# A fused attention and snake-MLP kernel whose whole order is exchanged, with its column sums taken from GpSimd back to TensorE

## The chip, the cores and the metric

The kernel runs on one core of a Trainium2 chip. The metric is the device time of one execution in microseconds (us), lower is better. Times are the median of three runs of the kernel before, 223.31 us (223.25 to 224.26).

## The reference

Eight batches of eight heads, 512 positions of 64 numbers, and 32 state rows for each head. Two attentions share their scores, and an MLP with a snake activation follows on all 4352 rows.

```python
def _attn_ref(x, state):                       # x 8x8x512x64, state 8x8x32x64
    scores = scale * np.matmul(x, state.transpose(0, 1, 3, 2))
    a = softmax(scores, -1);  xread = np.matmul(a, state)
    scores2 = scale * np.matmul(state, x.transpose(0, 1, 3, 2))
    a2 = softmax(scores2, -1);  sread = np.matmul(a2, x)
    return np.concatenate([xread, sread], axis=2)
def _moe_ref(x, w_in, w_out, alpha):           # x 4352x512, w_in 512x2048, w_out 2048x512
    h = x @ w_in
    s = np.sin(alpha * h)
    g = h + s * s / (alpha + 1e-09)
    return g @ w_out
```

## The kernel before

The core has five engines that run beside each other, each through its own list of instructions in order: TensorE (PE in the profile; its weight loads are PEld), VectorE (DVE), ScalarE (ACT), GpSimd (POOL), and SyncE (SP), which only issues DMAs here. An instruction that waits holds up everything behind it on its own engine. PE writes into PSUM, which has eight banks; a bank can be written anew once its last reader is done.

The kernel is a list of some 1,580 small steps, the text `ORDER`, written out by a search program. Each step is a method of the class `Steps`. There is no scheduler behind it: the steps are issued as they stand, so each engine gets its own steps in the order of the list. Steps of different engines that stand side by side in the list need not run at the same time.

A step is written as name, numbers, engine. `sq.3.8.A` is the step `sq` for batch 3 and column tile 8 on ScalarE (A; V is VectorE, G is GpSimd). Batches are numbered 0 to 7; the number 8 stands for the 256 state rows of all batches, which go through the MLP last. The 2048 hidden columns are 16 tiles f of 128. The steps that matter here, with their lines in the profile:

- `li`, `lo` (L287, L299): the four quarters of `w_in` and of `w_out` are loaded and made bf16, by DMAs that GpSimd issues. `lx.b` (L280): batch b of `x`, 512 KB in bf16, the same way. `pk.b` (L353): two copies that reorder it; both need the whole of `lx.b`. `td.b` (L394): a DMA on SP that transposes it.
- `sc` (L404): scores, two halves g of a batch. `ex` (L411): their exponential E on ScalarE. `rs`, `rr` (L415, L421): row sums and reciprocals on VectorE. `nm` (L205): the normalised scores A on GpSimd. `ad.b` (L445): a DMA on SP that transposes A of batch b into AT.
- `m.b.s` and `me` (L507, L515): M, the state of batch b times a quarter s of `w_in`, in two PSUM banks, and their two copies into SBUF. So the first matrix product of the MLP is AT times M, without xread ever being formed.
- `h.t.f.bank` (L556, two matmuls; `hg`, L574, is one of them; L562 for batch 8, four matmuls of half the width): hidden tile f of batch t. `si` (L582): its sine on ScalarE. `sq` (L205, or L591 on ScalarE): the square. `gt` (L598): the gate gT on VectorE, which reads the PSUM bank of h for the last time.
- `oo.t.st.bank` takes a bank, and `o.t.st.f` (L611) is one of the 16 matmuls that add up an output tile in it; `oc` (L619) copies it out and `os` (L626, L629) stores it by a DMA on SP. The last output tile, `oh.7.3`, is made in two pieces of 384 and 128 columns.
- `w.b` (L472, L480), `rc`, `xs` (L487, L490): the other attention. E is used unnormalised; its column sums over the 512 positions of a batch are needed beside it, spread over two halves of the partitions (r is 0 or 1).

The column sums are where the code differs. Before, GpSimd first adds the four token blocks of E: `ca` adds two pairs in float32 (L453), `cb` adds the results (L457), `ch` and `cl` split the sum in a high and a low bf16 part (L461, L465). Then four matmuls in `w` (L480) with a 128-column weight of zeros and ones, `sel`, add over the partitions.

```python
        for r in range(2):
            for p in range(2):
                Ev = k.t["hilo", b][:, p].rearrange("p g (h r j) -> p g h r j", h=2, r=2)
                k.nc.tensor.matmul(
                    wc[:, :, 2 * k.Ns:], k.sel[:, (1 - r) * k.D:(3 - r) * k.D], Ev[:, :, :, r],
                    start=(r == 0 and p == 0), stop=(r == 1 and p == 1),
                )
```

Of the kernel before, what the change touches and what calls it, by code (L numbers as in the profile page):

```python
# [10 lines left out]
ALU = mybir.AluOpType  # L11
AX = mybir.AxisListType
BF16 = mybir.dt.bfloat16
FP32 = mybir.dt.float32
U32 = mybir.dt.uint32
# [7 lines left out]
zero.1 identf.V lq.3.S s01_c.G s01_t.0 s01_k.1.A s01_k.0.V xq.0.V xq.1.A warm_up.4.512.7 xtq.1.0  # L23
l_st xtq.0.1 xq.2.V xq.3.V li.0 li.1 xc.0.0.0.V li.2 xtq.2.2 xc.0.1.0.V lo.0 xtq.3.3 lo.1 xc.0.0.1.A
sc.0.0.1 lx.1.0.1 xc.0.1.1.A li.3 ex.0.0 warm_up.1.512.7 sc.0.1.3 lo.2 ex.0.1 warm_up.1.512.7
st_t.1.1 rs.0.0 rr.0.0 nm.0.0.0.4.G ho.0.1.3 rs.0.1 rr.0.1 st_c.1.1.A st_c.1.0.V al_t.2 st_t.0.0
st_c.0.0.A warm_up.3.512.7 at.0.0.4 st_c.0.1.V m.0.0.1.5 sin_table ac.0.0.V me.0.0.0.V me.0.0.1.A
m.1.0.0.6 me.1.0.0.A nm.0.1.0.4.G at.0.1.4 ac.0.1.V lo.3 ho.0.3.7 hg.0.3.0 al_c inva hg.0.3.1 si.0.3
me.1.0.1.V lx.2.0.1 sq.0.3.V hg.0.1.0 hg.0.1.1 ho.0.2.0 hg.0.2.1 m.0.1.2.4 me.0.1.1.V si.0.1
sq.0.1.V me.0.1.0.A hg.0.2.0 si.0.2 sq.0.2.G ho.0.0.6 m.1.1.5.1 me.1.1.0.A hg.0.0.0 hg.0.0.1  # L30
ho.0.6.4 hg.0.6.1 gt.0.3 si.0.0 sq.0.0.G hg.0.6.0 me.1.1.1.A ho.0.5.2 hg.0.5.0 gt.0.1 hg.0.5.1
m.0.2.7.5 me.0.2.1.A gt.0.2 ho.0.7.3 hg.0.7.1 me.0.2.0.V ho.0.4.1 hg.0.4.1 hg.0.7.0 m.1.2.0.5 si.0.6
sq.0.6.G gt.0.0 me.1.2.1.A me.1.2.0.V hg.0.4.0 si.0.4 gt.0.6 sq.0.4.V gt.0.4 ho.0.10.7 hg.0.10.0
si.0.5 sq.0.5.G si.0.7 sq.0.7.G hg.0.10.1 ho.0.9.5 hg.0.9.1 hg.0.9.0 gt.0.5 ho.0.11.6 hg.0.11.0
oo.0.0.0 o.0.0.2 o.0.0.3 o.0.0.0 ca.0 cb.0 ch.0 hg.0.11.1 si.0.11 sq.0.11.V oo.0.3.4 o.0.3.1 o.0.3.3
si.0.9 sq.0.9.A o.0.3.2 o.0.3.0 o.0.0.1 oo.0.2.1 o.0.2.0 o.0.2.1 o.0.0.4 o.0.3.4 oo.0.1.2 o.0.1.2
o.0.1.6 o.0.0.6 o.0.1.4 o.0.1.1 o.0.3.6 o.0.2.3 gt.0.7 o.0.3.7 ho.0.8.3 hg.0.8.1 hg.0.8.0 o.0.3.5
gt.0.11 gt.0.9 si.0.10 sq.0.10.A gt.0.10 xt.1.1.5 xc.1.1.0.V xt.1.0.7 cl.0 si.0.8 pk.1.0.V
xc.1.0.1.V xc.1.0.0.V o.0.1.5 o.0.2.4 o.0.1.7 o.0.2.7 sq.0.8.A gt.0.8 xc.1.1.1.A sc.1.1.5 ex.1.1
o.0.2.5 m.0.3.7.6 me.0.3.0.V o.0.0.5 o.0.2.2 o.0.1.3 sc.1.0.3 ex.1.0 ho.0.15.7 o.0.2.6 me.0.3.1.V  # L40
hg.0.15.0 pk.1.1.V o.0.0.7 m.1.3.5.6 me.1.3.1.A rs.1.1 rr.1.1 nm.1.1.0.4.G hg.0.15.1 rs.1.0 rr.1.0
ho.0.13.3 hg.0.13.1 si.0.15 o.0.3.8 o.0.2.11 me.1.3.0.V o.0.3.11 o.0.0.10 hg.0.13.0 o.0.3.9
nm.1.0.0.4.G ad.1 o.0.1.10 sq.0.15.V o.0.2.8 o.0.0.8 gt.0.15 ho.0.14.5 o.0.1.8 hg.0.14.0 hg.0.14.1
ho.0.12.6 hg.0.12.1 hg.0.12.0 o.0.3.10 o.0.1.11 o.0.2.10 o.0.1.15 o.0.1.9 si.0.13 sq.0.13.G o.0.2.15
gt.0.13 lx.3.0.1 o.0.3.15 o.0.0.15 o.0.0.13 o.0.3.13 o.0.2.9 o.0.1.13 si.0.14 sq.0.14.A gt.0.14
o.0.0.14 o.0.0.11 si.0.12 sq.0.12.A o.0.2.14 o.0.1.14 o.0.0.9 gt.0.12 o.0.0.12 h.1.1.6 oc.0.0.A
h.1.15.5 pk.2.1.V pk.2.0.V td.2 si.1.1 si.1.15 h.1.14.0 si.1.14 sq.1.14.G h.1.12.3 sq.1.1.V o.0.3.12
sq.1.15.V h.1.6.7 o.0.1.0 si.1.12 gt.1.1 o.0.1.12 oc.0.1.A o.0.2.12 gt.1.15 si.1.6 o.0.3.14
sq.1.12.V oc.0.3.A h.1.13.6 sq.1.6.G si.1.13 h.1.2.2 o.0.2.13 oc.0.2.A h.1.4.5 si.1.4 si.1.2
pk.3.0.V oo.1.1.4 o.1.1.15 gt.1.14 gt.1.12 gt.1.6 o.1.1.1 sq.1.13.G sq.1.4.V lx.4.0.1 oo.1.2.0  # L50
o.1.2.14 o.1.2.1 o.1.2.15 o.1.1.12 h.1.7.3 si.1.7 sq.1.2.G sq.1.7.A h.1.11.7 h.1.9.1 o.1.1.14
gt.1.13 o.1.1.13 si.1.11 sq.1.11.G h.1.8.6 gt.1.4 o.1.1.4 oo.1.3.5 o.1.3.6 o.1.3.4 o.1.3.13 o.1.3.15
gt.1.7 o.1.3.7 si.1.9 gt.1.2 si.1.8 sq.1.8.G sq.1.9.A h.1.5.3 si.1.5 gt.1.11 o.1.3.1 h.1.10.2
si.1.10 gt.1.9 o.1.2.6 gt.1.8 sq.1.5.G os.0.2 o.1.2.13 os.0.1 h.1.3.7 o.1.1.9 si.1.3 h.1.0.1 si.1.0
sc.2.0.6 o.1.1.2 sq.1.10.G o.1.2.2 o.1.2.8 sq.1.3.G o.1.3.2 gt.1.5 o.1.2.9 o.1.2.7 ex.2.0 pk.3.1.V
o.1.3.8 o.1.1.7 gt.1.10 o.1.3.5 sc.2.1.2 ex.2.1 o.1.1.5 gt.1.3 o.1.2.12 rs.2.0 ca.1 o.1.2.4 rr.2.0
m.2.3.7.6 me.2.3.1.A me.2.3.0.A nm.2.0.0.4.G rs.2.1 rr.2.1 nm.2.1.0.4.G os.0.0 m.2.2.2.3 td.3
sq.1.0.A me.2.2.1.V o.1.2.10 cb.1 ch.1 o.1.2.3 me.2.2.0.A gt.1.0 o.1.1.3 oo.1.0.6 o.1.0.6 o.1.0.10
o.1.3.9 o.1.0.11 w.0.7 ad.2 o.1.0.5 o.1.2.11 rc.0 xs.0.0 o.1.0.3 xs.0.1 o.1.0.14 o.1.0.12 o.1.2.0
o.1.1.8 o.1.2.5 oc.1.2.V m.2.0.1.2 me.2.0.0.A m.2.1.7.3 me.2.0.1.V o.1.1.10 o.1.3.0 o.1.0.13  # L60
pk.4.1.V o.1.0.7 cl.1 pk.4.0.V me.2.1.0.A me.2.1.1.A sc.3.1.1 o.1.3.12 sc.3.0.7 ex.3.1 rs.3.1
o.1.3.11 rr.3.1 nm.3.1.0.4.G ex.3.0 rs.3.0 o.1.0.2 o.1.3.10 h.2.14.1 si.2.14 o.1.1.11 rr.3.0 td.4
nm.3.0.0.4.G o.1.1.6 o.1.3.3 o.1.3.14 h.2.6.7 oc.1.3.V o.1.1.0 h.2.15.3 oc.1.1.V si.2.6 h.2.11.5
o.1.0.8 sq.2.6.G si.2.11 si.2.15 h.2.3.4 si.2.3 sq.2.14.V gt.2.14 h.2.1.2 si.2.1 o.1.0.1 sq.2.11.V
sq.2.15.G gt.2.6 gt.2.11 sq.2.1.G h.2.4.1 si.2.4 sq.2.4.G h.2.7.0 gt.2.15 sq.2.3.V si.2.7 o.1.0.9
gt.2.1 gt.2.3 o.1.0.4 o.1.0.0 os.1.3 o.1.0.15 oc.1.0.A h.2.13.7 si.2.13 oo.2.3.5 o.2.3.11 os.0.3
gt.2.4 o.2.3.6 sq.2.13.G gt.2.13 o.2.3.14 h.2.5.3 h.2.10.6 si.2.5 o.2.3.15 oo.2.1.2 o.2.1.6 o.2.1.15
sq.2.7.A si.2.10 o.2.1.1 sq.2.5.A h.2.9.4 si.2.9 ad.3 h.2.2.1 si.2.2 sq.2.2.A o.2.3.3 gt.2.7 gt.2.5
o.2.1.14 sq.2.10.G gt.2.10 h.2.12.7 sq.2.9.G gt.2.9 gt.2.2 w.1.0 h.2.8.3 o.2.3.5 o.2.3.13 o.2.1.4
o.2.1.13 o.2.1.5 sc.4.1.4 si.2.8 h.2.0.6 sq.2.8.A rc.1 si.2.12 si.2.0 oo.2.0.1 o.2.1.11 o.2.0.2  # L70
sq.2.12.V o.2.0.3 o.2.3.7 o.2.0.10 o.2.0.4 o.2.0.13 gt.2.12 o.2.0.9 o.2.3.1 gt.2.8 ex.4.1 xs.1.0
o.2.3.12 o.2.0.14 sq.2.0.G o.2.0.12 xs.1.1 o.2.3.9 m.3.0.4.3 m.3.1.0.7 o.2.1.2 ca.2 me.3.0.1.A cb.2
ch.2 gt.2.0 me.3.0.0.V o.2.3.4 o.2.3.8 me.3.1.1.A o.2.0.0 sc.4.0.4 o.2.3.10 ex.4.0 o.2.1.8
me.3.1.0.V m.3.3.0.7 m.3.2.3.6 rs.4.1 rr.4.1 h.3.0.4 o.2.3.0 o.2.0.5 me.3.3.0.V me.3.3.1.A o.2.0.1
nm.4.1.0.4.G o.2.0.6 me.3.2.1.A cl.2 o.2.1.0 me.3.2.0.V oo.2.2.3 o.2.2.14 o.2.2.3 rs.4.0 rr.4.0
si.3.0 h.3.12.6 si.3.12 nm.4.0.0.4.G o.2.3.2 h.3.8.0 o.2.0.7 h.3.9.7 oc.2.3.V sq.3.12.V gt.3.12
os.2.3 lx.5.0.1 si.3.8 sq.3.8.V si.3.9 gt.3.8 sq.3.0.V gt.3.0 h.3.4.5 sq.3.9.G gt.3.9 o.2.2.1 si.3.4
o.2.1.12 o.2.0.8 h.3.13.6 si.3.13 sq.3.13.A gt.3.13 o.2.1.9 o.2.2.7 sq.3.4.G o.2.2.6 os.1.2 gt.3.4
ad.4 o.2.2.0 h.3.3.0 si.3.3 o.2.0.11 o.2.0.15 o.2.1.10 oc.2.0.A sq.3.3.G gt.3.3 h.3.11.4 o.2.1.7
si.3.11 sq.3.11.G os.1.0 gt.3.11 o.2.1.3 o.2.2.5 oc.2.1.A os.2.1 h.3.7.1 si.3.7 sq.3.7.G o.2.2.8  # L80
m.4.3.6.7 me.4.3.1.V m.4.2.2.5 me.4.2.0.A pk.5.0.V gt.3.7 o.2.2.11 me.4.2.1.A h.3.15.0 si.3.15
o.2.2.15 me.4.3.0.A o.2.2.2 h.3.14.4 h.4.9.5 si.3.14 oo.3.3.7 sq.3.15.V gt.3.15 h.3.5.2 si.3.5
# [607 lines left out]
```

## Time and profile before

| what | before |
| --- | --- |
| median of 3 runs | 223.31 us (223.25 to 224.26) |
| the profiled execution, own time | 224.26 us |
| its span in the profile | 222.2 us |
| TensorE busy | 210.7 us, 95% of the span |
| VectorE busy | 179.3 us, 81% |
| ScalarE busy | 167.8 us, 76% |
| GpSimd busy | 109.9 us, 49% |
| granted TensorE clock, mean | 0.998 |
| DMA, mean | 106 GB/s |
| last matmul starts | 218.62 us after the start of the span |

The span is the time from the first to the last instruction of the program in one profiled execution; the device time has some 2 us around it. The profile names, for an engine's idle time, what ended it ("<-"). A mean over the whole span hides that this kernel has stages: up to 18 us it waits for weights, then it runs through the batches, and the end is a chain of output tiles.

### The profile page before, as it was taken

Reading aid. Unit: us, or ns where it says so; the run is one execution under the profiler, and the core shown is the slowest. Engines: PE = TensorE matmul, PEld = TensorE weight load, DVE = VectorE, ACT = ScalarE, POOL = GpSimd, SP = SyncE. Lnnn points to the kernel's source line nnn. Section 1 sums busy time; section 2 is a strip of 40 time slices with the busy share of each in tenths; the row PEclk is TensorE's granted clock in tenths of the full one; section 3 lists DMA queues with packets and bytes.
Section 4 is the critical chain, followed back from the end, with each engine's and each line's share of the span. In section 5 each row is a group of like instructions: output and inputs, shape, how many; then the busy total and the mean of one; then the engine's idle time right before and its main releaser. Section 6 shows DMA issues by size and latency. Waiting matters only on the chain.

```text
span 222.2 us, 4123 instructions
## 1 busy us (share of the span) xinstructions
PE 210.7 (95%) x1507; PEld 101.1 (46%) x1535; DVE 179.3 (81%) x325; ACT 167.8 (76%) x280; POOL 109.9 (49%) x126
## 2 busy tenths in 40 slices
PE   7888899999999999699999999999999999999993
PEld 2533444444444534244444444444553556565452
DVE  4698997699999998799999687998888897676422
ACT  3698688899599989867998689986976669673510
POOL 5956706288658467645356274801280543620100
PEclk9999999999999999999999999999999999999999
DMA  6999995978583004919715332651023200320044
GB/s 181 186 206 203 205 203 87 179 159 128 95 157 82 0 3 77 217 37 238 98 47 97 94 94 24 121 118 71 4 65 124 97 0 7 138 97 0 0 145 142
DMA packets 38052, 23.48 MB, mean 106 GB/s; under 512 B 20992, under 2 KB 33680, under 8 KB 38032
## 3 DMA queue, kind: packets, MB, share of 16 engines
q1 hardware_dynamic: 26128, 15.08, 26.3%
q0 software_dynamic: 11648, 8.13, 25.7%
q8 instruction: 12, 0.20, 0.3%
q14 instruction: 8, 0.07, 0.1%
q10 hardware_dynamic: 256, 0.01, 0.1%
HBM read 17.44 MB, written 8.91 MB: 119 GB/s over the span
## 4 chain that ended last, share of the span: by engine, by line
PE 79%; DMA 10%; DVE 3%; ACT 2%; POOL 2%; issue 1%; SPq 0%; ACTq 0%
PE o_ps L611 47%; PE h_ps L556 20%; DMA w_in_sb<-in_moe_w_in_dram 6%; DMA AT<-A 4%; PE m_ps L507 3%; PE h_ps L562 3%; DVE gT L598 2%; PE w_ps L472 2%; PE s_ps L404 1%; DMA s<-in_state_dram 1%; ACT M L515 1%; DVE s L205 1%; ACT s L582 1%; PE h_ps L574 1%; PE w_ps L480 1%
## 5 line engine op out<-in xcount | busy, mean ns | idle before, releaser
L611 PE MATMUL o_ps<-w_out_sb,gT 128*128 128x512 bf16 (+2 forms) x541 | 135.1, 373 | 1.9 <-issue 0.6
L598 DVE SCALAR_TENSOR_TENSOR gT<-s,inva_sb,h_ps 128x512 bf16<-128x512 bf16 (+1 forms) x144 | 98.7, 714 | 13.4 <-POOL s L205 8.2
L582 ACT ACTIVATE s<-h_ps,alpha_sb 128x512 bf16<-128x512 f32 (+1 forms) x144 | 90.1, 665 | 21.6 <-PE h_ps L556 11.0
L205 POOL TENSOR_TENSOR s<-s 128x512 bf16<-128x512 bf16 (+1 forms) x55 | 55.2, 1011 | 69.2 <-ACT s L582 68.5
L611 PEld LDWEIGHTS <-gT 128*128 128x128 bf16 x560 | 52.2, 98 | 61.3 <-issue 4.9
L556 PE MATMUL h_ps<-AT,M 128*128 128x512 bf16 x218 | 61.3, 379 | 2.5 <-DMA AT<-A 1.9
L556 PEld LDWEIGHTS <-M 128*128 128x128 bf16 x224 | 21.5, 98 | 27.0 <-ACT s L582 2.4
L205 DVE TENSOR_TENSOR s<-s 128x512 bf16<-128x512 bf16 (+1 forms) x51 | 23.2, 455 | 6.1 <-ACT s L582 5.5
L205 POOL TENSOR_TENSOR A<-E,rR 128x512 bf16<-128x512 bf16 x16 | 16.6, 1055 | 22.4 <-ACT E L411 9.3
L515 ACT CAST M<-m_ps 128x512 bf16<-128x512 f32 x37 | 20.2, 592 | 8.5 <-PE m_ps L507 8.4
L591 ACT ACTIVATE s<-s 128x512 bf16<-128x512 bf16 (+1 forms) x38 | 23.2, 613 | 1.0
L619 ACT COPY o_sb<-o_ps 128x512 f32<-128x512 f32 (+1 forms) x24 | 13.8, 576 | 13.0 <-PE o_ps L611 13.0
L515 DVE CAST M<-m_ps 128x512 bf16<-128x512 f32 x27 | 17.7, 676 | 3.5 <-PE m_ps L507 3.4
L619 DVE COPY o_sb<-o_ps 128x512 f32<-128x512 f32 (+1 forms) x11 | 7.3, 674 | 6.9 <-PE o_ps L611 6.8
L415 DVE TENSOR_REDUCE R<-E 128x16 f32<-128x512 bf16 x16 | 10.6, 661 | 2.7 <-ACT E L411 2.7
L507 PE MATMUL m_ps<-w_in_sb,stT 64*32 64x512 bf16 x256 | 10.7, 382 | 1.4 <-DMA w_in_sb<-in_moe_w_in_dram 1.2
L411 ACT ACTIVATE E<-s_ps 128x512 bf16<-128x512 f32 x16 | 9.0, 600 | 1.6 <-PE s_ps L404 1.6
L453 POOL TENSOR_TENSOR sum<-E 128x512 f32<-128x512 bf16 x8 | 9.4, 1175 | 0.2
L562 PE MATMUL h_ps<-xs_all,w_in_sb 128*128 128x256 bf16 x64 | 9.3, 273 | 0.1
L574 PE MATMUL h_ps<-AT,M 128*128 128x512 bf16 x30 | 8.7, 381 | 0.3 <-DVE M L515 0.3
L353 DVE COPY xp<-xnat 128x1024 bf16<-128x1024 bf16 x14 | 7.0, 510 | 1.5 <-DMA xnat<-in_x_dram 1.5
L562 PEld LDWEIGHTS <-w_in_sb 128*128 128x128 bf16 x64 | 6.3, 98 | 3.4 <-DVE xs_all L490 0.2
(62 smaller groups left out, 122.6 us busy)
## 6 DMA issues: line engine op xcount, KB each, us to landing
out_dram<-o_sb SPq DMA_DIRECT2D x33, 256.0 KB, 2.7
xnat<-in_x_dram POOLq DMA_DIRECT2D x7, 512.0 KB, 8.8
w_in_sb<-in_moe_w_in_dram POOLq DMA_DIRECT2D x4, 512.0 KB, 11.0
w_out_sb<-in_moe_w_out_dram POOLq DMA_DIRECT2D x4, 512.0 KB, 18.5
x<-in_x_dram SPq DMA_DIRECT2D x4, 256.0 KB, 3.8
st_nat<-in_state_dram POOLq DMA_DIRECT2D x1, 256.0 KB, 5.7
out_dram<-o_sb SPq DMA_DIRECT2D x1, 192.0 KB, 2.3
s<-in_state_dram SPq DMA_DIRECT2D x1, 128.0 KB
```

Of the source, the lines that this page charges most:

```text
L205: {"V": k.nc.vector, "G": k.nc.gpsimd}[eng].tensor_tensor(out, a, b, ALU.mult)
L415: k.nc.vector.reduce_sum(R[:, g], k.t["E", b][:, g].rearrange("p c (h j) -> p (c h) j", j=k.Ns), axis=AX.X)
L507: k.nc.tensor.matmul(k.t["m", b, s + n, g][o0:o0 + k.Ns, :], k.stT[k.half(r), b * k.G + g, c0:c0 + k.Ns], k.w_in_sb[k.half(r), 2 * g + h, ...
L515: k.copy(eng)(k.t["M", b][:, g, s * k.FW:(s + 1) * k.FW], k.t["m", b, s, g][:])
L556: k.nc.tensor.matmul(hp[:, :n], k.t["M", t][:, g, fs], k.t["AT", t][:, g, :], start=(g == 0), stop=(g == k.G - 1),)
L562: k.nc.tensor.matmul(hp[:, :n], k.w_in_sb[:, q, fs], k.xs_all[:, q].rearrange("p b j -> p (b j)"), start=(q == 0), stop=(q == k.Q - 1),)
L574: k.nc.tensor.matmul(k.t["h", t, f][:], k.t["M", t][:, g, f * k.P:(f + 1) * k.P], k.t["AT", t][:, g, :], start=k.made["h", t, f] == 1, sto ...
L582: k.nc.scalar.activation(s[:, :n], k.t["h", t, f][:, :n], ACT.Sin, scale=k.alpha_sb[:, f:f + 1])
L591: k.nc.scalar.activation(s2[:, :n], s[:, :n], ACT.Square)
L598: k.nc.vector.scalar_tensor_tensor(gT[:, :n], k.t["s2", t, f][:, :n], k.inva_sb[:, f:f + 1], k.t["h", t, f][:, :n], ALU.mult, ALU.add,)
L611: k.nc.tensor.matmul(k.t["o", t, st, half][:, cols], k.t["gT", t, f][:, rows], k.w_out_sb[:, f, cols], start=k.made["o", t, st, half] == 1 ...
L619: k.copy(eng)(o_sb[:, cols], k.t["o", t, st, half][:, cols])
```

## The change

The functions change little. `ca`, `cb`, `ch` and `cl` go, with their two pools; `sel` becomes `ones`, 64 columns wide. A new step `cs.b` stands on its own, apart from `w.b`, and adds E itself over tokens and partitions by eight matmuls on TensorE, which use 64 of the array's columns each, by turns the first and the second half.

```diff
-        k.nc.vector.memset(k.sel[:].bitcast(U32), 0)
-        k.nc.vector.memset(k.sel[:, k.D:2 * k.D], 1.0)
+        k.nc.vector.memset(k.ones[:], 1.0)
...
-    def ca(k, b):
...
-    def cl(k, b):
...
-        for r in range(2):
-            for p in range(2):
-                Ev = k.t["hilo", b][:, p].rearrange("p g (h r j) -> p g h r j", h=2, r=2)
+
+    def cs(k, b):
+        E, wc = k.t["E", b], k.t["w", b]
+        for i in range(k.C):
+            for r in range(2):
+                Ev = E[:, :, i, :].rearrange("p g (h r j) -> p g h r j", h=2, r=2)
                 k.nc.tensor.matmul(
-                    wc[:, :, 2 * k.Ns:], k.sel[:, (1 - r) * k.D:(3 - r) * k.D], Ev[:, :, :, r],
-                    start=(r == 0 and p == 0), stop=(r == 1 and p == 1),
+                    wc[k.half(r), :, 2 * k.Ns:], k.ones[:], Ev[:, :, :, r],
+                    start=(i == 0), stop=(i == k.C - 1),
                 )
```

The list `ORDER` is exchanged as a whole. Counted over it, these numbers of steps change; all others are equal:

| step | before | after |
| --- | --- | --- |
| `ca`, `cb`, `ch`, `cl` on GpSimd | 8 each | none |
| `cs` on TensorE (8 matmuls each) | none (4 matmuls in each `w`) | 8 |
| `sq` on GpSimd / ScalarE / VectorE | 55 / 38 / 51 | 43 / 46 / 55 |
| `me` on ScalarE / VectorE | 37 / 27 | 38 / 26 |
| `oc` on ScalarE / VectorE | 23 / 10 | 21 / 12 |
| copies `s01_k`, `st_c` on ScalarE / VectorE | 3 / 3 | 5 / 1 |
| warm-up matmuls | 14 | 15 |
| the loads on GpSimd's queue, up to `lx.2` | | same order |

The order around the fifth load of `x`, which the prediction speaks of, before (first) and after (second); lines are cut where a "..." stands:

```
... rs.4.0 rr.4.0 si.3.0 h.3.12.6 si.3.12 nm.4.0.0.4.G ... oc.2.3.V sq.3.12.V gt.3.12
os.2.3 lx.5.0.1 ... o.2.2.6 os.1.2 gt.3.4
ad.4 ... os.1.0 ... os.2.1 ... me.4.2.0.A pk.5.0.V gt.3.7 ... h.3.14.4 h.4.9.5 ...
```

```
... sc.4.1.2 rr.4.0 m.3.2.3.0 m.3.3.4.5 ex.4.1 o.2.3.8 rs.4.1 me.3.3.0.A me.3.3.1.A rr.4.1 nm.4.1.0.4.G
me.3.2.0.V o.2.0.0 ... oc.2.3.V os.2.3 h.3.1.5 si.3.7 sq.3.7.V gt.3.7 ... h.3.14.6 si.3.1 ... si.3.15
sq.3.1.V sq.3.15.V h.3.8.4 si.3.8 sq.3.8.A o.2.0.9 gt.3.1 ... nm.4.0.0.4.G gt.3.15
si.3.14 sq.3.14.V gt.3.14 o.2.0.3 h.3.10.2 si.3.10 sq.3.10.A gt.3.10 gt.3.8 o.2.2.13 lx.5.0.1
pk.5.1.V o.2.2.8 o.2.2.2 h.3.0.5 si.3.0 sq.3.0.V ... gt.3.0 ... h.3.5.4 o.2.1.3 os.1.1 os.1.2
h.3.2.5 os.1.3 o.3.3.15 os.1.0 ... ad.4 ... h.4.13.7 ...
```

On SP's own queue the stretch is `td.4 os.1.3 os.0.3 ad.3 os.2.3 os.1.2 ad.4 os.1.0 os.2.1` before and `td.4 ad.3 os.2.3 os.1.1 os.1.2 os.1.3 os.1.0 ad.4 os.2.0` after. On GpSimd's it is `nm.4.1 cl.2 nm.4.0 lx.5` before and `nm.4.1 nm.4.0 lx.5` after. The end of the list is `oh.7.3.0 ... oh.7.3.1` (the piece of 384 columns first) before, and `oh.7.3.1 ... oh.7.3.0` after.

## The prediction

> **What bounds the kernel now.** I read the page first, for the share of each engine and the chain that ended last.
>
> ```profile
> PE 210.7 (95%) x1507; PEld 101.1 (46%) x1535; DVE 179.3 (81%) x325; ACT 167.8 (76%) x280; POOL 109.9 (49%) x126
> ...
> PE 79%; DMA 10%; DVE 3%; ACT 2%; POOL 2%; issue 1%; SPq 0%; ACTq 0%
> ```
>
> TensorE is the bound, GpSimd is half idle. So taking work from GpSimd buys nothing by itself, and giving TensorE work costs its full price. What matters is how many microseconds TensorE loses. Second, the groups of instructions, for the sums and for the narrow matmuls that the new ones resemble.
>
> ```profile
> L381 PE MATMUL x_ps<-ident,xnat 128*64 128x128 bf16 x32 | 1.3, 220 | 0.1
> L480 PE MATMUL w_ps<-hilo,sel 128*128 128x128 bf16 x32 | 3.1, 219 | 0.0
> ```
>
> "128*64" is a matmul on half of the array's columns. Both last 0.22. The chain has sixteen of L381 in 0.64, so they start (0.64 - 0.22) / 15 = 0.028 apart (0.0275 in the trace); those of L480 start 0.056 apart. Two half-width matmuls thus run together in the time of one full. Third, the timeline of TensorE around a group of `m`.
>
> ```profile
> 142.28 0.81 PE L611 MATMUL o_ps<-w_out_sb,gT 128*128 128x512 bf16 x3
> 143.02 0.62 PE L507 MATMUL m_ps<-w_in_sb,stT 64*32 64x512 bf16 x16
> 143.58 1.25 PE L611 MATMUL o_ps<-w_out_sb,gT 128*128 128x512 bf16 x5
> ```
>
> Full matmuls start 0.216 apart (three end 0.81 after the first starts, one takes 0.38). The third `o` starts at 142.71, so `m` comes 0.31 later: 0.093 more than the spacing. The same 0.09 is lost going back. It is the price of a change of array shape. Last, the timeline from 84 to 95, where the longest loss is.
>
> ```profile
> 84.41 0.94 POOL L280 DMA_DIRECT2D xnat<-in_x_dram  x1
> 84.72 0.81 SPq L626 DMA_DIRECT2D out_dram<-o_sb  x2
> 85.70 1.38 SPq L445 DMA_TRANSPOSE AT<-A  x1
> 93.85 1.25 DVE L353 COPY xp<-xnat 128x1024 bf16<-128x1024 bf16 x1 [1.51 <-DMA xnat<-in_x_dram]
> 94.45 1.46 PE L556 MATMUL h_ps<-AT,M 128*128 128x512 bf16 x6 [1.92 <-DMA AT<-A]
> ```
>
> Load `lx.5`, stores and transpose `ad.4` are issued within 3 us. The transpose lands after 8.6 (median of its kind 3.1), the load after 9.4. VectorE stands 1.5, TensorE 1.9.
>
> **The floor before.** Until 17.99 TensorE waits for the third quarter of `w_in` (landing 17.95); the loads have the same order after, so both kernels start there with `m.0.2`. From there the list has 528 full `o` and 244 `h` matmuls at 0.216 (166.8), the `o` in pieces (16 x 0.162, 16 x 0.054: 3.5), 64 of `h.8` at 0.109 (7.0), 28 groups of `m` at 0.216 (6.0), 240 short ones at 0.029 (7.0), 32 sums at 0.056 (1.8), 32 transposes (0.9): 192.9. With 33 changes of shape at 0.093 (3.1) the last matmul could start at 213.9. It starts at 218.62: TensorE loses 4.7. Counted along the trace: 1.4 by 28 us, 2.1 by 86, 4.3 by 94.5, 4.7 at the end. From that start to the end of the span pass 3.6.
>
> **The change, part by part.**
>
> *Sums.* GpSimd loses 32 steps (9.4 + 6.0 + 3.6 + 5.5 = 24.5 us): no wait of TensorE for them stands in the waits, so the gain is zero. TensorE has 64 matmuls at 0.0275 (1.76) for 32 at 0.056 (1.79): even. But they change the array's shape. Some `cs` stand beside an `m` or another `cs`; counted over the list there are 41 changes for 33: +0.75. One `hg` more falls after `m.0.2`: +0.2. I take the last piece off again (384 columns, so its start is 0.11 earlier): the last start's floor is 214.7, 0.8 later.
>
> The Trainium skill has a rule against the change here: by "TensorEngine Tiling (Array Packing)", Key Properties, changing the tiling mode drains TensorE. It gives no duration; the row's 0.093 is what I have, and without any drain the sum would be 0.75 less.
>
> *Squares.* 12 leave GpSimd, 8 go to ScalarE (0.61 each, 4.9) and 4 to VectorE (0.455, 1.8): 173 and 181 of 222 us. Both stay under TensorE: zero, if no stage is overfull; the walk below has such a stage.
>
> *VectorE beside GpSimd.* VectorE's squares and `pk` copies take 0.42, but up to 1.28 while a GpSimd step runs; ten stretched ones have 3.7 us too much in all. After, 44 of 103 such GpSimd steps are gone. That is VectorE's time, not TensorE's; I take zero, with a bound of 0.9 of gain, the one stretched square (21.57) that the chain passes through.
>
> "SBUF — State Buffer" of the skill (SBUF: two separate sides; the shared port pair is an exclusive lock) has the blocked one wait for a whole GpSimd step; the trace shows less than one step each time, 0.07 to 0.86, and scaled by 44 of 103 the rule's effect would be 1.6 us of VectorE.
>
> *18 to 32 us.* I walked the queues with the rows' durations. `hg.0.11` needs bank 5, after two copies on VectorE (0.67 each) that follow `m.1.2`: 0.6 lost. `m.0.3` waits 0.15 for a copy on ScalarE, `hg.0.12` and `m.1.3` 0.25 for `ex` behind its table load (1.28). Sum 1.0, where 1.4 was lost: −0.4.
>
> *The transpose `ad.4`.* `h.4.13` comes at floor 96.9, `ad.4` can go at 85.6: 11 us and more. Even 8.6 fits: −2.1.
>
> *The load `lx.5`.* This decides. With 1.6 lost by then `sc.4.1` starts at 79.6 (floor 78.0); `ex` ends 80.6, `rs`, `rr` (0.66, 0.25) 81.55, `nm.4.1`, `nm.4.0` (1.05 each) 83.7: there `lx.5` goes. `oc.2.3` ends 83.3, so SP issues `os.2.3` at 83.4, and then the four `os.1`, long ready behind it, at 0.45 apart, and `ad.4`: five stores and a transpose on the same DMA engines. In VectorE's queue `pk.5.1` needs the load. Before it: ScalarE's three copies and table load end 83.7, `si.3.7` 84.4, then on VectorE four squares (0.42) and six gates (0.75) to 90.6. Behind it: `sq.3.0`, `gt.3.0`, which frees bank 5 for `h.3.2`, due at 91.7 on TensorE. In time, `gt.3.0` ends 90.6 + 0.42 + 0.42 + 0.75 = 92.2: 0.5 lost. The load's rows: 5.9, 6.4 and 5.8 with no store beside it, 8.8 with three stores, 9.4 here. So a store adds 1.0, and five give up to 10.9. I take 9.4, the row with stores and a transpose; bounds 5.8 and 10.9. Then `gt.3.0` ends 83.7 + 9.4 + 1.6 = 94.7: 3.0 lost (0.5 to 4.5). The stores' own landing has no reader that is near.
>
> *Elsewhere.* The other four loads and the transposes keep their distances to their readers within 3 us and have no stores beside them; I leave the 0.7 lost from 28 to 86 and the 0.4 after 94.5 as they are. Bounds: 1 less, 1 more.
>
> *The end.* The last piece is now 384 columns: matmul end 0.1 later, copy 0.47 (between 0.27 for 128 and 0.58 for 512), landing 2.3 for 2.1.
>
> ```profile
> 218.14 1.43 SPq L626 DMA_DIRECT2D out_dram<-o_sb  x3
> 218.88 0.27 ACT L619 COPY o_sb<-o_ps 128x128 f32<-128x128 f32 x1 [6.15 <-PE o_ps L611]
> ```
>
> With the last store landing 2.1 after its issue before, together +0.5: 4.1 behind the last start.
>
> **Sum.** 214.7 + 1.0 + 0.7 + 3.0 + 0.4 + 4.1 = 223.9 against a span of 222.2: +1.7. The profiled execution's own time is 224.26, 1 us over the median of 223.31; the difference goes onto the median: 225.0 (onto the own time, 226.0). Under 0.5%, 1.1 us, a measurement of this kernel cannot tell from no change.
>
> **Rivals.**
>
> *The load is in time* (faster or even). If `lx.5` lands within 6.9 us of its issue, VectorE never stands, 0.5 is lost in place of 3.0, and the span is 221.4: 222.5. For it: the load is issued 0.3 after the first store, so its packets could go ahead of four of five. Against: 8.8 with three stores issued within 0.9 of it.
>
> *All the queues fit* (faster). The new order loses nothing but 1.0 at 18 to 32 and 0.5 later: 214.7 + 1.5 + 4.1 = 220.3, or 221.4. For it: GpSimd is emptier, and its squares come back sooner. Against: ScalarE and VectorE carry more, and the order before lost 0.7 even in the quiet stretch from 28 to 86. Faster by over 0.5% takes total losses below 2.3 us.
>
> *It doesn't do what it says* (slower still). The order is said to know of stores that share the queues, yet the list sends four at once behind a fifth, beside a load. If each store adds its full 1.0, the loss is 4.5 and the time 226.5.
>
> **How the numbers follow.** The load late: 0.55, from 224.0 (landing 8.8, 0.4 less elsewhere) to 226.5 (landing 10.9), of which 0.40 over 224.4 and 0.15 within 0.5%. In time: 0.20, split 0.09 faster, 0.11 same. All fits: 0.20, faster. Worse elsewhere: 0.05, 0.04 slower. So faster 0.29, same 0.27, slower 0.44. The range, 221.2 to 226.5, leaves out only the best of the fitting case and the worst elsewhere.
>
> **What would show it.** Right: a wait of VectorE for `xnat` of 2 us or more near 91 to 94, TensorE idle near 92 to 95 behind a gate, no wait for AT there, changes of shape around the sums at 0.09, a last copy near 0.47. Wrong: `lx.5` landing within 7 us, or waits of several us on TensorE anywhere else.

## The result, and the profile after

| what | before | after |
| --- | --- | --- |
| median | 223.34 us (222.45 to 224.26, 6 runs) | 229.45 us (228.16 to 230.29, 6 runs) |
| ratio, with its 95% interval | | 1.0266 (1.0222 to 1.0309) |
| profiled execution, own time / span | 224.26 / 222.2 us | 228.51 / 226.4 us |
| granted TensorE clock, mean over the six executions of after | | 0.983 to 0.993 |
| TensorE loses, from `m.0.2` to the last start | 4.7 us | 8.1 us |
| last store behind the last matmul's start | 3.6 us | 3.7 us |

The changed kernel is 6.1 us slower, outside the forecast range (221.2 to 226.5). The ratios, here and below, leave out executions that took over 1.5% longer than the fastest of the same kernel, and the medians have all of them, so a ratio need not be the quotient of two medians. Line numbers have moved: `h` is now L539, `gt` L581, `o` L594, `pk` L350, `lx` L277, `os` L609, `ad` L442, the square on VectorE or GpSimd L203, the sums `cs` L463.

The page of after, first the engines' busy times, then the clock row, then the chain that ended last.

```profile
PE 213.6 (94%) x1540; PEld 103.9 (46%) x1568; DVE 177.5 (78%) x327; ACT 171.2 (76%) x289; POOL 74.5 (33%) x82
...
PEclk9999999999999999979999999999999999999998
...
PE 76%; DVE 9%; DMA 6%; ACT 5%; issue 2%; POOL 0%; SPq 0%
```

GpSimd fell from 109.9 to 74.5 us, and VectorE a little, but the chain spends less of its share on TensorE (76% for 79%) and three times as much on VectorE. In the clock row one slice (each is 5.7 us) has a 7: the clock was not full there (the 8 at the end is the time after the last matmul). The profile records what share of the full clock TensorE was granted: it fell to half at 95.47 us and came back at 98.88. The profiled execution of before had no such slice.

The waits of after; after the line stand the total, the number of waits and the longest.

```profile
DVE xp L350 <- DMA xnat<-in_x_dram: 4.6, 1, 4.6
PE h_ps L539 <- DVE gT L581: 4.5, 1, 4.5
```

One wait of each, and they are one event. The timeline of after from 78 to 100 us (start, duration, engine, line, what it does; in brackets the idle time before, and what ended it):

```profile
82.22 2.69 SPq L609 DMA_DIRECT2D out_dram<-o_sb  x5
82.88 0.94 POOL L277 DMA_DIRECT2D xnat<-in_x_dram  x1
85.02 2.94 SPq L442 DMA_TRANSPOSE AT<-A  x1
93.32 0.43 DVE L350 COPY xp<-xnat 128x1024 bf16<-128x1024 bf16 x1 [4.62 <-DMA xnat<-in_x_dram]
94.92 0.59 PE L539 MATMUL h_ps<-AT,M 128*128 128x512 bf16 x2 [4.54 <-DVE gT L581]
96.92 2.86 PE L594 MATMUL o_ps<-w_out_sb,gT 128*128 128x512 bf16 x8
```

SP issues five stores and a transpose within 3 us, and GpSimd the load `lx.5` among them. The load lands 10.4 us after its issue. VectorE stands at `pk.5.1` for 4.6 us, `gt.3.0` stands behind it, and TensorE has idled 4.5 us when `h.3.2` starts at 94.92. The last line shows what follows: eight matmuls take 2.86 us, where at full clock seven spacings of 0.216 and one of 0.38 make 1.9.

The column sums of after, from the timeline of TensorE from 49 to 57:

```profile
54.84 0.63 PE L452 MATMUL w_ps<-E,xp 128*128 128x64 bf16 x16
55.40 0.41 PE L463 MATMUL w_ps<-E,ones 128*64 128x128 bf16 x8
55.74 1.47 PE L594 MATMUL o_ps<-w_out_sb,gT 128*128 128x512 bf16 x6
```

Eight sums start 0.028 apart, as taken from the old rows. Each group starts 0.094 later than the spacing, and what follows it 0.12 later. The forecast had 0.093 for both. (For `m`, the rows that the forecast shows have the same: 0.56 us pass from the start of `m` at 143.02 to the next `o`, where two groups of 0.216 take 0.43, so the way out costs 0.13.)

### The profile page after: what moved, and what is told of

The parts are those of the page before. It is cut to its first block, busy times and chain, and to the rows that moved or that the text cites. A ratio compares the mean times of both kernels' runs of the same rounds, so it can differ in the third digit from the quotient of the medians.

```text
span 226.4 us, 4152 instructions
## 1 busy us (share of the span) xinstructions
PE 213.6 (94%) x1540; PEld 103.9 (46%) x1568; DVE 177.5 (78%) x327; ACT 171.2 (76%) x289; POOL 74.5 (33%) x82
## 4 chain that ended last, share of the span: by engine, by line
PE 76%; DVE 9%; DMA 6%; ACT 5%; issue 2%; POOL 0%; SPq 0%
PE o_ps L594 44%; PE h_ps L539 17%; DMA xnat<-in_x_dram 5%; DVE gT L581 4%; PE h_ps L557 3%; PE m_ps L490 3%; PE h_ps L545 3%; PE s_ps L401 2%; ACT s L565 2%; DMA x<-in_x_dram 1%; DVE s L203 1%; DVE rC L470 1%; DVE M L498 1%; PE w_ps L452 1%; PE x_ps L363 1%
## 5 line engine op out<-in xcount | busy, mean ns | idle before, releaser
L594 PE MATMUL o_ps<-w_out_sb,gT 128*128 128x512 bf16 (+2 forms) x542 | 138.5, 376 | 1.6 <-issue 0.5
L581 DVE SCALAR_TENSOR_TENSOR gT<-s,inva_sb,h_ps 128x512 bf16<-128x512 bf16 (+1 forms) x144 | 98.1, 714 | 13.6 <-ACT s L574 8.1
L565 ACT ACTIVATE s<-h_ps,alpha_sb 128x512 bf16<-128x512 f32 (+1 forms) x144 | 90.4, 668 | 20.8 <-PE h_ps L539 13.0
L594 PEld LDWEIGHTS <-gT 128*128 128x128 bf16 x560 | 52.3, 98 | 60.6 <-issue 5.2
L203 POOL TENSOR_TENSOR s<-s 128x512 bf16<-128x512 bf16 (+1 forms) x43 | 44.2, 1035 | 99.3 <-ACT s L565 93.5
L539 PE MATMUL h_ps<-AT,M 128*128 128x512 bf16 x216 | 62.3, 381 | 4.6 <-DVE gT L581 4.5
L539 PEld LDWEIGHTS <-M 128*128 128x128 bf16 x224 | 21.8, 98 | 30.4 <-issue 6.1
L203 DVE TENSOR_TENSOR s<-s 128x512 bf16<-128x512 bf16 (+1 forms) x55 | 22.5, 411 | 8.4 <-ACT s L565 8.1
L203 POOL TENSOR_TENSOR A<-E,rR 128x512 bf16<-128x512 bf16 x16 | 16.5, 1047 | 34.8 <-ACT M L498 14.6
L574 ACT ACTIVATE s<-s 128x512 bf16<-128x512 bf16 (+1 forms) x46 | 27.2, 592 | 0.9
L602 ACT COPY o_sb<-o_ps 128x512 f32<-128x512 f32 (+1 forms) x22 | 12.8, 586 | 16.8 <-PE o_ps L594 16.7
L498 DVE CAST M<-m_ps 128x512 bf16<-128x512 f32 x26 | 16.9, 674 | 1.1 <-PE m_ps L490 0.9
L602 DVE COPY o_sb<-o_ps 128x512 f32<-128x512 f32 (+1 forms) x13 | 8.4, 653 | 6.6 <-PE o_ps L594 6.4
L350 DVE COPY xp<-xnat 128x1024 bf16<-128x1024 bf16 x14 | 6.0, 438 | 4.7 <-DMA xnat<-in_x_dram 4.6
L557 PE MATMUL h_ps<-AT,M 128*128 128x512 bf16 x31 | 8.5, 380 | 0.5 <-ACT M L498 0.5
L470 DVE RECIPROCAL rC<-w_ps 128x128 f32<-128x128 f32 x8 | 7.5, 944 | 1.5 <-PE w_ps L463 1.4
## 6 DMA issues: line engine op xcount, KB each, us to landing
w_in_sb<-in_moe_w_in_dram POOLq DMA_DIRECT2D x4, 512.0 KB, 10.4
```

The source lines that it names most:

```text
L203: {"V": k.nc.vector, "G": k.nc.gpsimd}[eng].tensor_tensor(out, a, b, ALU.mult)
L498: k.copy(eng)(k.t["M", b][:, g, s * k.FW:(s + 1) * k.FW], k.t["m", b, s, g][:])
L539: k.nc.tensor.matmul(hp[:, :n], k.t["M", t][:, g, fs], k.t["AT", t][:, g, :], start=(g == 0), stop=(g == k.G - 1),)
L557: k.nc.tensor.matmul(k.t["h", t, f][:], k.t["M", t][:, g, f * k.P:(f + 1) * k.P], k.t["AT", t][:, g, :], start=k.made["h", t, f] == 1, sto ...
L565: k.nc.scalar.activation(s[:, :n], k.t["h", t, f][:, :n], ACT.Sin, scale=k.alpha_sb[:, f:f + 1])
L574: k.nc.scalar.activation(s2[:, :n], s[:, :n], ACT.Square)
```

## The experiments

The kernel before ran beside each set (medians 223.49 to 223.61). "Half clock" counts the executions with a mean clock under 0.995; a whole half-clock stretch (3.41 us at half, so 1.7 us lost) takes the mean to some 0.992.

| kernel | median, us | ratio (95%) | `lx.5`, issue to landing | TensorE idle before `h.3.2` | half clock |
| --- | --- | --- | --- | --- | --- |
| after | 229.45 | 1.0266 (1.0222 to 1.0309) | 10.41 | 4.54 | 6 of 6 |
| `e1` copy later | 223.32 | 0.999 (0.996 to 1.0021) | 10.45 | none | 0 of 10 |
| `e2` stores early | 227.33 | 1.0112 (1.0068 to 1.0156) | 7.98 | 3.59 | 5 of 10 |
| `e3` zeros in the wait | 227.86 | 1.0136 (1.0075 to 1.0197) | 10.42 | filled | 0 of 4 |
| `f4` ten zeros | 228.38 | 1.0167 (1.0107 to 1.0227) | 10.57 | 2.31 | 4 of 6 |
| `f2` transpose late | 231.33 | 1.026 (1.0167 to 1.0352) | 9.65 | 3.56 | 6 of 6 |
| `f3` stores early, transpose late | 223.21 | 0.998 (0.9949 to 1.001) | 5.96 | none | 0 of 12 |

**Is it this one wait?** `e1` moves a single step: the first of the load's two copies goes next to the second, behind the gates that TensorE needs.

```diff
-lx.5.0.1 pk.5.1.V o.2.2.8 ... os.2.2 pk.5.0.V td.5
+lx.5.0.1 o.2.2.8 ... os.2.2 pk.5.1.V pk.5.0.V td.5
```

> The changed kernel with one step moved: the copy pk.5.1 goes behind gt.3.3 on VectorE, just ahead of pk.5.0. Theory 1 (a copy that waits for lx.5 holds VectorE, its gate holds bank 5, TensorE stands 4.5 us and then runs 3.4 us at half clock): the wait of VectorE for xnat falls from 4.6 to under 1 us, the idle time of TensorE before h.3.2 and the half clock are both gone, the span falls by about 6 us to 220.3, and the time lies near 222.5, below the kernel before. Rival (the new order is worse in many places and this one only the most visible): something else stands in the same stretch, and the span falls by under 3 us, to 223.5 or more.

Timeline of `e1`, 85 to 97:

```profile
85.09 2.76 SPq L442 DMA_TRANSPOSE AT<-A  x1
...
91.35 0.59 PE L539 MATMUL h_ps<-AT,M 128*128 128x512 bf16 x2
...
94.75 1.60 DVE L350 COPY xp<-xnat 128x1024 bf16<-128x1024 bf16 x2
```

The load lands no earlier (10.45), but both copies find it there and no wait stands in brackets. Median 223.32: 6.1 us less than after, and no different from before. So the whole difference between the two medians hangs on the place of one copy in VectorE's queue. The span came to 221.2, 0.9 over what I had expected.

**Why is the load late?** `e2` lets SP issue the four `os.1` behind `ad.3`, 16 to 18 us earlier (64.4 to 68.6). `f2` moves the transpose `ad.4` behind `os.2.2`. `f3` moves the stores as `e2`, and `ad.4` behind `os.2.0`.

```diff
-... ad.3 ... os.2.3 ... os.1.1 os.1.2 ... os.1.3 ... os.1.0 ... ad.4 ... os.2.0 ... os.2.2
+... ad.3 os.1.2 os.1.1 os.1.0 os.1.3 ... os.2.3 ... ad.4 ... os.2.0 ... os.2.2       (e2)
+... ad.3 ... os.2.3 ... os.1.1 os.1.2 ... os.1.3 ... os.1.0 ... os.2.0 ... os.2.2 ad.4   (f2)
+... ad.3 os.1.2 os.1.1 os.1.0 os.1.3 ... os.2.3 ... os.2.0 ad.4 ... os.2.2       (f3)
```

> The changed kernel with the four stores os.1 moved ahead of os.2.3 on SP's queue, to behind ad.3, some 18 us earlier; pk.5.1 stays where it is. Theory 1a (the load is late because five stores share the DMA engines with it, 1 us each): lx.5 lands 6 to 7.5 us after its issue in place of 10.4, VectorE waits 0.5 to 1.5 us, TensorE stands about 1 us before h.3.2, the clock stays at 1.0, and the span is 221 to 222. Rival (the transpose ad.4, or the load itself, makes it late): lx.5 still takes 9 us or more, and the span stays over 224.5.

> After, with the four os.1 behind ad.3 (as in the run with stores early) and also ad.4 behind os.2.0, so that lx.5 has only the end of one store beside it. If the load is late because of what shares the DMA engines: it lands within 6.0 to 6.8 us of its issue, VectorE's wait for xnat falls from 4.6 to under 1.0, TensorE's wait ahead of h.3.2.5 to 0.5 to 1.0, no half clock there; span 226.4 - 4.0 - 1.7 = 220.5 to 221.5, median 222.5 to 223.5. Rival (something in VectorE's own queue holds the gate): the load lands early, the wait ahead of h.3.2.5 stays over 2, span over 223.

> After, with ad.4 moved behind os.2.2 alone, so that lx.5 has the five stores beside it, but no transpose. Measured so far: 5.96 with neither, 7.98 with the transpose alone, 10.4 with both. If stores and transpose each add their part: about 10.4 - 2.0 = 8.2 to 8.8, the wait of VectorE 2.5 to 3, TensorE's ahead of h.3.2.5 2.5 to 3, half clock in half of the executions; span 223.5 to 225, median 225.5 to 227. Rival (the transpose only fills what the stores leave): 10 or more, median as after, 229. Rival (stores cost nothing without a transpose): under 7, median 223.5.

Together with after they make a table of two by two: 5.96 us with neither, 7.98 with the transpose alone, 9.65 with the stores alone, 10.41 with both. The stores cost 3.7 alone, the transpose 2.0, both 4.5. They do not add up in full, and my expectation for `f2` (8.2 to 8.8) was wrong: the stores are the larger part. Each figure is from one profiled execution, but the two ends come again in others: 10.45, 10.42 and 10.57 in `e1`, `e3` and `f4`, and 5.98 in `g1` below, which has the stores and the transpose of `f3`. Two things are not held equal in this table. One store, `os.2.3`, goes out just ahead of the load in all four kernels, so "the stores" are the other four. And in `e2` the transpose goes out 0.1 us behind the load, in after 2.1 us behind it.

`e2` gained less than its load did. Its timeline of VectorE from 89 to 95:

```profile
90.75 1.07 DVE L350 COPY xp<-xnat 128x1024 bf16<-128x1024 bf16 x1 [2.20 <-DMA xnat<-in_x_dram]
91.74 1.25 DVE L203 TENSOR_TENSOR s<-s 128x512 bf16<-128x512 bf16 x1
93.03 2.06 DVE L581 SCALAR_TENSOR_TENSOR gT<-s,inva_sb,h_ps 128x512 bf16<-128x512 bf16 x3
```

and GpSimd's over the same stretch:

```profile
89.41 3.30 POOL L203 TENSOR_TENSOR s<-s 128x512 bf16<-128x512 bf16 x3 [5.73 <-ACT s L565]
```

The copy and the square took 0.43 and 0.42 in after, where GpSimd's three squares lay inside VectorE's wait (89.55 to 92.67). In `e2` the load landed 2.6 us earlier, in the midst of them, and the two steps took 1.07 and 1.25. So 1.5 of the gain was lost again while GpSimd was at work. That is the price of VectorE beside GpSimd which the forecast had put at zero for TensorE.

`f2` shows a new wait in place of the old (timeline, 90 to 108):

```profile
93.67 0.59 PE L539 MATMUL h_ps<-AT,M 128*128 128x512 bf16 x2 [3.56 <-DVE gT L581]
...
99.62 1.30 SPq L442 DMA_TRANSPOSE AT<-A  x1
...
104.73 1.03 PE L539 MATMUL h_ps<-AT,M 128*128 128x512 bf16 x2 [2.07 <-DMA AT<-A]
```

`os.2.2`, behind which I put `ad.4`, waits for an output tile that is itself late. So the transpose went out at 99.6 in place of 85, `h.4.13` waited 2.1 for it, and four of the six executions had the half clock twice. `f3`, with both apart (timeline, 82 to 97):

```profile
83.05 0.94 POOL L277 DMA_DIRECT2D xnat<-in_x_dram  x1
...
89.03 0.43 DVE L350 COPY xp<-xnat 128x1024 bf16<-128x1024 bf16 x1 [0.17 <-DMA xnat<-in_x_dram]
```

The wait falls to 0.17. Its median is that of `e1`: whether the load comes early or its copy stands late makes no difference.

**What does the half clock cost, and what brings it?** `e3` and `f4` put 20 or 10 matmuls with a zero operand into TensorE's wait, added into an open output tile.

```diff
-... o.2.1.3 os.1.1 os.1.2 h.3.2.5
+... o.2.1.3 os.1.1 os.1.2 fill.2.1.20 h.3.2.5        (f4: fill.2.1.10)
```

> The changed kernel with 20 matmuls of zeros (4.3 us of TensorE) put ahead of h.3.2 and added into the output tile 2.1, which they leave as it is; the wait for lx.5 stays. Theory 2 (the clock is halved because TensorE stood idle for 4.5 us): h.3.2 starts as late as before, but the clock stays at 1.0 behind it, so the span falls by 1.7 us to about 224.7. Rival (the half clock has another cause, or comes by time): the clock falls all the same and the span is 226.4 or more.

> After, with ten matmuls of a zero operand added into the open sum of o.2.1 ahead of h.3.2.5 (twenty in the run before this one). They take 2.2 us of the 4.5 of idle time, and leave 2.3 in one piece. If it is the length of the idle time that brings the half clock, most executions keep the full clock (4 of 5, as before did with 2.1 us idle; after had it in 6 of 6, and the run with 3.5 us idle in 4 of 10): median 229.4 - 1.6 + 0.3 = 228.1. Rival (any wait at this place, or the mean work of TensorE in the stretch): half clock in most executions, median 229 or more.

The wait itself stays in `e3`: VectorE stands for 4.63 us, as the timeline shows.

```profile
91.88 4.48 PE L601 MATMUL o_ps<-warm 128*128 128x512 bf16 x20
94.77 0.43 DVE L350 COPY xp<-xnat 128x1024 bf16<-128x1024 bf16 x1 [4.63 <-DMA xnat<-in_x_dram]
96.37 0.59 PE L539 MATMUL h_ps<-AT,M 128*128 128x512 bf16 x2
```

But the clock stays full in all four executions, and the median falls by 1.6, which is the price of the half clock (1.7 in the trace). The profiled execution of `e3` has a span of 226.2, hardly under after's, but all of it comes 1.4 us later from the first transposes on (`ad.1` at 34.84 for 33.40), far ahead of the edit; the second and third quarter of `w_in` landed later in it (15.5 and 18.0 us for 13.9 and 17.3). `lx.5` and `h.3.2` come 1.4 later too, so what follows `h.3.2` is 1.7 us shorter than in after.

In `f4` (timeline of TensorE, 90 to 98) the ten end before the gate does:

```profile
90.10 2.32 PE L601 MATMUL o_ps<-warm 128*128 128x512 bf16 x10
94.73 1.01 PE L539 MATMUL h_ps<-AT,M 128*128 128x512 bf16 x2 [2.31 <-DVE gT L581]
```

It leaves 2.31 us idle, and I expected the full clock in four of five executions (from counts that were too low: `e2` had the half clock in five of ten, not four). It fell in four of six. So an idle stretch much shorter than 3.4 us is enough.

**What does the code cost by itself?** `f1` has the order of before, with `ca`, `cb`, `ch` and `cl` taken out of the list, and `cs.b` put behind `w.b`.

```diff
-... ca.0 cb.0 ch.0 ... cl.0 ... w.0 rc.0
+... w.0 cs.0 rc.0
```

> The order of before, with the functions of after: ca, cb, ch, cl are taken out of the list, and cs.b stands right behind w.b. The code part alone. My price: eight groups of eight matmuls at 0.0275 in place of 32 at 0.056 (even), and at most 16 more changes of shape at 0.094 with those of w gone: floor +0.75, span 222.2 + 0.75 = 223.0 or less; the emptier GpSimd gives VectorE up to 1.6 us, of which I take 0 to 0.5 on TensorE. Median 223.6 + 0.3 to 0.8 = 223.9 to 224.4 (ratio 1.001 to 1.004). Rival (the sums cause the loss of after): ratio over 1.01. Rival (GpSimd was the hidden limit): ratio under 0.995.

Measured: 224.79 us, ratio 1.0068 (1.0032 to 1.0104), so 1.2 us for 0.3 to 0.8 expected. I had miscounted: behind `w` every group of sums brings two changes of shape of its own, 16 x 0.093 = 1.5, where the new order saves half of them by putting `cs` beside `m` or another `cs`. The losses of TensorE fell by 0.4 (4.4 for 4.7), perhaps through the emptier GpSimd, so 1.5 - 0.4 = 1.1 stands against 1.2 measured. (At the 0.094 in and 0.124 out that the trace of `f1` shows, the sixteen changes cost 1.7.) Since `f1` is 1.2 over before and `f3` even with it, the new order, without its one misplaced wait, earns back what the new sums cost; by which of its moves, no run shows.

`g1` takes the sums back the other way: the order of `f3` with the functions of before, and `ca` to `cl` put by hand onto GpSimd's queue, 5 to 110 steps ahead of `w`.

> The order of the run with stores early and transpose late, but the column sums taken back: the functions of before, cs out of the list, and ca, cb, ch, cl of each batch put onto GpSimd's queue 5 to 110 steps ahead of its w. The new order with the old sums. If the price of the sums is the changes of shape: TensorE's floor falls by 0.75 to 1.2, VectorE and the squares on GpSimd come somewhat later (0.4 in the run with the old order and the new sums): 223.2 - 0.4 to 0.8 = 222.4 to 222.8, ratio 0.994 to 0.997. Rival (squares and scores queue behind the sums on GpSimd, gates come late): 223.2 or more.

230.15 us, ratio 1.0323 (1.0266 to 1.0379). The loss comes late (timeline, 160 to 170):

```profile
164.24 1.15 POOL L453 TENSOR_TENSOR sum<-E 128x512 f32<-128x512 bf16 x1
...
166.42 1.41 DVE L598 SCALAR_TENSOR_TENSOR gT<-s,inva_sb,h_ps 128x512 bf16<-128x512 bf16 x2 [3.27 <-POOL s L205]
167.22 0.63 PE L507 MATMUL m_ps<-w_in_sb,stT 64*32 64x512 bf16 x8 [4.21 <-DVE gT L598]
```

A square stands behind my sums on GpSimd, a gate waits 3.3 us for it, TensorE 4.2. The rival came true, but through my placing, so this run does not say what a well-placed old sum would be worth in the new order.

**A better version.** The same two things, in the order of before. `e4` moves `lx.5` behind `sq.3.3.G` and sets its copies together. `f5` moves the copies and `td.5` behind `gt.3.1` too. `g2` sets `lx.5` behind `sq.3.11.G` and the copies behind `gt.3.10`; `g3` has `lx.5` of `g2` and the copies of `f5`.

```diff
-os.2.3 lx.5.0.1 ... gt.3.4 ad.4 ... sq.3.3.G ... sq.3.11.G ... pk.5.0.V ... pk.5.1.V ... td.5 ... gt.3.1
+os.2.3 ... gt.3.4 ad.4 ... sq.3.3.G ... sq.3.11.G lx.5.0.1 ... gt.3.1 pk.5.0.V pk.5.1.V td.5        (g3)
```

> The kernel before with its own clash parted: lx.5 goes behind sq.3.3 on GpSimd's queue, about 5.5 us later, and pk.5.0 goes next to pk.5.1. Theory 1 (load, stores and transpose ad.4 in one stretch are what costs 2.1 us there): ad.4 lands within 4.5 us, TensorE no longer stands before h.4.9, the span falls from 222.2 to about 220.2 and the time to about 221.3, so that the old order without its clash is as good as the new one without its own or better. Rival (another wait takes its place): VectorE waits for xnat before the copies and the span stays within 0.7 of 222.2.

> Before, with lx.5 behind sq.3.3.G (as in the fourth run) and its two copies pk.5.0, pk.5.1 and td.5 moved behind gt.3.1, so that no gate stands behind the wait for the load. In the fourth run VectorE's wait (1.25) and the copies (1.0) held gt.4.9, which frees bank 5 for h.3.10.5, and TensorE lost 1.41. If that is all: span 220.4 - 1.4 = 219.0, median 223.0 - 1.4 = 221.6, ratio 0.990. Rival (gt.4.9 is held by the square on GpSimd or by ScalarE): loss at h.3.10.5 stays over 0.8, ratio 0.994 or more.

> The run of before with the load's copies behind the gates, with lx.5 now behind sq.3.11.G and the two copies and td.5 behind gt.3.10. There h.3.14.4 lost 0.75, because gt.3.11 waited 0.91 for its square, which stood behind the 0.94 of issuing lx.5 on GpSimd. If that is all, the loss goes: 222.1 - 0.6 = 221.5, ratio 0.989. Rival (the square comes late from ScalarE's sine anyway): loss at h.3.14.4 stays over 0.5, median 222.0.

> The run of before with the load's copies behind the gates (222.07), with lx.5 moved behind sq.3.11.G, while the copies stay behind gt.3.1 (in the run before this one they went behind gt.3.10, and held me.4.0 and with it h.4.6.4 for 0.75). There lx.5 landed at 95.9, and the copies stood at 98.4, so the load is in time. Losses of 3.35 fall by the 0.75 at h.3.14.4: 222.1 - 0.6 = 221.5, ratio 0.988 to 0.990. Rival (single losses of under 1 us drown in the spread of executions, as with the run before this one): 222.0 to 223.0, and no better than the run with the copies behind the gates.

| kernel | median, us | ratio (95%) |
| --- | --- | --- |
| `e4` load later | 223.02 | 0.9954 (0.992 to 0.9987) |
| `f5` copies behind the gates | 222.07 | 0.9917 (0.9888 to 0.9946) |
| `g2` square ahead of the load, copies behind `gt.3.10` | 222.99 | 0.9969 (0.9937 to 1.0001) |
| `g3` square ahead of the load, copies behind `gt.3.1` | 220.84 | 0.9883 (0.9831 to 0.9936) |

In `e4` the span (220.4) came as expected, the median did not; VectorE still waited 1.25 for the load, and TensorE lost 1.41 at `h.3.10`. In `f5` that is gone, and one place is left (timeline, 86 to 93.5):

```profile
89.10 0.94 POOL L280 DMA_DIRECT2D xnat<-in_x_dram  x1
...
91.16 0.75 DVE L598 SCALAR_TENSOR_TENSOR gT<-s,inva_sb,h_ps 128x512 bf16<-128x512 bf16 x1 [0.91 <-POOL s L205]
...
91.95 1.89 PE L556 MATMUL h_ps<-AT,M 128*128 128x512 bf16 x8 [0.59 <-DVE gT L598]
```

Issuing a load occupies GpSimd for 0.94 us, and the square behind it makes a gate, and then TensorE, late. `g2` removes that, but its later copies hold `me.4.0` and cost 0.75 at `h.4.6`, and 0.64 more is lost behind a gate at 104.7. It gained nothing over `f5`; its median is even 0.9 higher, and its profiled execution (221.92), one of its fastest, does not show the whole reason. `g3` does the one without the other. Of 4.7 us lost before, 1.9 are left; its span is 218.2 and its median 1.2% under before (six executions), the fastest of all. Of the 4.0 us between the two spans 1.1 isn't the order's: the third quarter of `w_in` landed at 16.8 in this execution, and at 17.95 in that of before. The medians differ by 2.65.

## Why the prediction was wrong

By its own steps, on the profiled execution:

| term of the sum | predicted | measured |
| --- | --- | --- |
| floor of the last start | 214.7 | 214.6 |
| lost up to 86 us | 1.7 | 0.65 |
| the load `lx.5` | 3.0 | 4.5 |
| half clock | not in the sum | 1.7 |
| lost later | 0.4 | 1.2 |
| behind the last start | 4.1 | 3.7 |
| span | 223.9 | 226.4 |
| from the profiled execution to the median | -0.95 | +0.94 |

The forecast of 225.0 fell 4.45 us short. By these rows 1.7 of it is the half clock, 1.9 the step from the profiled execution to the median, 0.8 the later losses, and 0.45 the load together with what was lost ahead of it; the end gave 0.4 back. The two steps that failed are the price of an idle TensorE and the step to the median. Taking away either one alone leaves the time over 226.5 (227.7 or 227.6).

**The load.** This term was mis-sized, 3.0 for 4.5. Place, mechanism and rows were right: `lx.5` went at 82.9 (83.7 forecast), `gt.3.0` ended at 94.86 (94.7). But the working "9.4, the row with stores and a transpose" took a row with three stores beside the load for a list with five. It landed after 10.4, inside the bound of 10.9, and TensorE lost the 4.5 that stood as the upper end. That the end of the wait fitted is luck: the stages ahead had lost 1.05 less than forecast (0.2 for 1.0 at 18 to 32 us, and 0.5 for 0.7 after), so the load went out 0.8 early, which nearly made up for the 1.0 that it took longer. Of the 1.5 more that TensorE lost, 1.0 is the longer load, and 0.5 is that TensorE reached `h.3.2` 1.3 early (90.4 for 91.7), the load only 0.8. Adding the losses ahead of the wait to the wait was right in kind, because the issue of `lx.5` hangs, over `nm.4.0`, on TensorE's own scores: in `e3` TensorE came 1.4 later, the load went out 1.4 later, and VectorE's wait stayed at 4.63.

**The half clock.** The forecast knew no price for an idle TensorE beyond the idle time. It is 1.7 us per occurrence, and `e3` removes it alone. This is the mechanism that was missed: the range had no term for it.

The Trainium skill has it: "TensorE: Matmul & The Clock Gate", Part 1, describes a gate that watches a free-running window of 3413 ns and halves the clock after an idle one. The traces agree on the window: the stretches of full clock in after last 85.33 and 126.29 us, 25 and 37 times 3.413, and the half one 3.413. They differ on the idle time: the page's section on oscillation warns of gaps over some 3.4 us, while here 2.31 (`f4`) and 2.07 (`f2`) brought a drop; the measurement decides.

**Later.** Besides the half clock 0.8 more was lost than forecast. 0.17 of it stands at `m.7.2`, whose two groups take 0.80 us there (0.81 in `e1`) and 0.63 elsewhere. Some 0.3 is the way out of the changes of shape, which costs 0.12 and not 0.093; the rest lies in small steps that I have not traced.

**From profile to median.** The profiled execution of before was 0.95 above its median, and I took that off. The one of after is 0.94 below. That is 1.9 of the 4.45 us by which the forecast fell short; 2.5 are the span. I read a single execution's distance as a property of the program. Of what makes the other executions of after longer, the clock shows a part: two have a mean clock of 0.983 or 0.984, for a second half-clock stretch.

**What held.** The wait at `AT` for `ad.4` is gone (2.1 before, none in after), though `ad.4` still landed only after 8.9 us. No wait of TensorE came with the squares that moved to ScalarE and VectorE. VectorE's squares fell from 455 to 411 ns and its copies from 510 to 438 with the emptier GpSimd; what TensorE gained from it is not shown (`f1`, the old order with the emptier GpSimd, lost 0.4 less). The sums were even but for the changes of shape. The Trainium skill's "TensorEngine Tiling (Array Packing)", Key Properties, which has a change of tiling mode drain TensorE, agrees with the 0.094 and 0.12 here, and with the 1.2 us of `f1`. The last copy took 0.48 (0.47).

**The rivals.** "It doesn't do what it says" came true in its mechanism, with four stores at once behind a fifth and 4.5 lost, at 226.5 in my sum for 229.45 measured. "The load is in time" is what `f3` makes of it, 223.2 for 222.5, and `e1` gets as far with the load still late. "All the queues fit" (221.4) did not come even in these two, which have no such wait.

## What to carry to other kernels

A load that shares the DMA engines with a burst of stores can take 1.6 times its time (9.65 us for 5.96), and 1.75 times with a transpose beside them, so look at what else is issued in the 3 us around it. But the cheapest cure is on the reader's side: put the instruction that waits for it behind everything that the bottleneck engine needs from the same queue (and see what stands behind it there: in `g2` the copies held the next step up). Price a stall of TensorE with the clock that it may lose, here 1.7 us on top of a 4.5 us wait. And ask what the issue of a late load hangs on: here it hangs on TensorE's own work, so time lost ahead of it moves the load and its reader together. Last, the distance of one profiled execution from the median is no property of a program: it was +0.95 before and -0.94 after.

## What was not expected of the hardware

The clock of TensorE is decided on a fixed grid. In the traces a drop always comes at a whole number of windows of 3.413 us from the moment the clock was first granted (25.0 in after and `f4`, 26.0 in `e2` and `f2`, 47.0 in `g1`, and 63.0 in before, for the end of work), and lasts one window, or two. Counting TensorE's idle time within each window: the windows that ended in a drop while work went on had 1.84 (`f2`), 2.14 (`f4`), 2.81 (`f2`), 2.87 (after), 2.91 (`e2`) and 3.02 us (`g1`) of it; windows with 1.81 (`e3`) and 1.92 (before) had none, and neither had one with 1.84 near the end of `f2`. So every window with 2.1 us or more idle ended in a drop, none under 1.8 brought one on, and in between the idle time alone doesn't tell; what else counts there is open. What brings the clock back is open too: in `g1` the drop held for a second window, though only 1.19 us of the first were idle. Whether a wait of 2 to 3.6 us crosses this depends on how it falls on the grid. That fits its appearing in only some executions of `f4` (4 of 6) and `e2` (5 of 10). Before, with its one wait of 1.9 us, had it in 17 of the 80 executions that ran beside the experiments; why in these is open, since no trace of one was taken.
